# Attention with sinks and a window, then a gated feed-forward: token blocks of the feed-forward re-cut, two groups' attention placed later

## The chip, the cores and the metric

The kernel runs on one core of one Trainium2 chip. The metric is the time of one execution on the device in microseconds (us). Five engines work beside each other, each through its own list of instructions in the order in which it was written: TensorE (PE; its weight loads are shown as PEld), VectorE (DVE), ScalarE (ACT), GpSimd (POOL) and SyncE (SP). Loads that change the type are issued by POOL, transposing transfers and most stores by SP, some stores by ACT.

## The reference

Causal attention over 4 batches, 8 heads, 768 positions, head size 64. A query sees the last 128 positions (its own included) and the first 4, the sinks. The attention's output, 3072 tokens of 512, goes through a gated feed-forward of width 1536.

```python
scores = scale * np.matmul(q, k.transpose(0, 1, 3, 2))
keep = is_sink | in_window            # rel >= 0 and rel < 128, or position < 4
a = np.exp(scores - max); a = a / sum # masked scores are -1e9
x = (a @ v).transpose(0, 2, 1, 3).reshape(B * S, H * D)
g = x @ w_gate
out = (g * sigmoid(g) * (x @ w_val)) @ w_out
```

## The kernel before

**Groups and blocks.** The attention works in 12 *groups* of 256 tokens (three for each batch; group g holds tokens 256 g on). The feed-forward works in 8 *blocks* whose sizes stand in `SIZES` (L42); the first two are gated together. `gate` (L611) is one unit of the first half: a projection `pg` into one PSUM bank (`project`, L564: 4 matmuls of 512 columns, or 8 of 256), its tanh on ACT (L584), a projection `pv` into another bank, then on DVE `u` (L592) and `ht` (L607). A block of 512 has 12 gate units, one of 256 has 6. `down` (L644) is one unit of the second half: 12 matmuls (L657) for 128 tokens, an eviction on ACT (L662) and a store (L665).

**A group's attention.** `load_nat` (L106) brings q and k with four transfers from POOL into a tile of which there is one (`natp`, one buffer); `xbar` (L287) turns them into `kT` and `qT` with four transposing transfers from SP (L293). `step_S1` (L360) writes the scores of all heads into six PSUM banks (L382; 52 matmuls, or 18 for a batch's first group) and, except where it is called "apart", the sinks' scores into a seventh (L432), and has ACT take the exponent of three banks (L395). `step_S2` (L408) takes that of the other three and of the sinks; `step_S1`, `step_S2` and `step_S3` append the four masks, multiplications on DVE (L404), to the list `later`. `step_PV` (L469) multiplies by the values: the first call of a group that has sinks runs `step_sinks` (L447), which opens all four output banks, adds the sinks (L454) and, with L463, the odd parts of the window for all eight heads; every call then adds the main part (L494) and appends a division on DVE (reciprocal L503, product `xn` L511). `step_X` (L523) has SP transpose `xn` into `xT`, the feed-forward's input (L538).

**The order of the work.** The schedule is written by hand: `weave` (L714) runs a list of units and hands each one its attention steps; the numbers in the slots are positions in that list. Within a gate unit, steps marked "ahead" (`step_S1`) come before `pg`, the others between `pg` and `pv`; within a down unit they are spread over its 12 matmuls. `flush` (L241) writes out what `later` holds; in a gate unit `gate_v` (L590) may first put reciprocals, or one mask if it is the first entry, between `u` and `ht`. PSUM has 8 banks, handed out from one pool (L76). POOL's order is kept by `behind` (L701) and `turned` (L705): one-element copies that wait for a transposed tile, so that loads issued behind them start no sooner.

**Around the change.** The first list has 24 units: 12 of gates for blocks 0 and 1, 6 for block 2 (12 to 17), and the downs of blocks 0, 1, 2 (18 to 23). Group 3 is scored at unit 17 and its PVs stand in 19 and 20; group 4 is scored at 19, its PVs stand in 21 and 22. Block 3 (512 tokens) then holds groups 3 and 4; its first two gate units work on 256 tokens each, so that group 4's half may come later. From there on `pair(a, b)` puts two groups into each block's list: a's scores at unit 0, its PVs at 4 and 5, its `step_X` at 7, b's scores at 8, its PVs at 12 and 13, its `step_X` at 13. Block 3 has groups 5 and 6, block 4 has 7 and 8, block 5 has 9 and 10; group 11 is worked while blocks 6 (512) and 7 (256) are gated, and the downs of both follow.

Of the kernel before, what the change touches and what calls it, by code (L numbers as in the profile page):

```python
# [14 lines left out]
def kernel(  # L15
# [12 lines left out]
    nc = tc.nc  # L28
    P = 128
# [9 lines left out]
    NP2 = H // 2  # L39
    GC = S // 256  # L40
    NG = B * GC
    SIZES = [256, 256, 256, 512, 512, 512, 512, 256]  # L42
    assert sum(SIZES) == NTOK and NG == 12
    OFF = [sum(SIZES[:i]) for i in range(len(SIZES))]
    PEX = (0, 1, 2)
# [34 lines left out]
    def bank(shape, dtype, name):  # L80
        return psum.tile(shape, dtype, tag="b", name=name)
# [102 lines left out]
    one = const.tile([P, 1], FP32)  # L184
# [56 lines left out]
    def flush():  # L241
        firsts()
        for f in later:
            f()
        later.clear()
# [274 lines left out]
    def dense(t, c, n):  # L520
        return t[:, 0:c * n].rearrange("p (c n) -> p c n", c=c)

    def step_X(g, j, evict="v"):  # L523
        t0 = g * 256 + j * P
        tb = max(i for i in range(len(SIZES)) if OFF[i] <= t0)
        off = t0 - OFF[tb]
        if tb == 0 and off == 0:
            xTs["01"] = xtp.tile([P, DMC, 512], BF16, tag="xT", name="xT")
            xTs[0], xTs[1] = (xTs["01"][:, :, 256 * i:256 * (i + 1)] for i in range(2))
        elif tb > 1 and off == 0:  # L530
            xTs[tb] = dense(xtp.tile([P, DMC * 512], BF16, tag="xT", name="xT"),
                            DMC, SIZES[tb])
            if tb == 3:
                for i in range(2):
                    xTs[tb, i] = xTs[tb][:, :, 256 * i:256 * (i + 1)]
        if g not in PEX:
            def sp():
                nc.sync.dma_start_transpose(xTs[tb][:, :, off:off + P], xns[g, j])  # L538
            later.append(sp)
            return  # L540
        pt = bank([P, DMC, P], BF16, "px")
        for i in range(DMC):
            nc.tensor.transpose(pt[:, i], xns[g, j][:, i * P:(i + 1) * P], ident)  # L543

        if evict == "a":
            nc.scalar.copy(out=xTs[tb][:, :, off:off + P], in_=pt)
            return

        def dve():
            nc.vector.tensor_copy(out=xTs[tb][:, :, off:off + P], in_=pt)  # L550
        if evict == "now":
            dve()
        else:
            later.append(dve)
# [18 lines left out]
    def new_h(tb):  # L573
        if tb not in hts:
            n = SIZES[tb]
            t = hpool.tile([P, DFC * 512], BF16, tag="ht", name="ht")
# [13 lines left out]
    def gate_v(tb, f, pg, th, pv):  # L590
# [11 lines left out]
        if tb == "01":  # L602
# [4 lines left out]
        nc.vector.tensor_tensor(  # L607
            hts[tb][:, f:f + 512 // SIZES[tb]].rearrange("p a n -> p (a n)"), u, pv,
            op=ALU.mult)
# [23 lines left out]
    def gate_first(tb, f, attn):  # L633

        step_PV(1, 0, 1, "a")
        step_PV(1, 1, 1)
        flush()
        a = gate_a(tb, f)
        step_X(1, 1, "now")
        step_X(1, 0, "a")  # L640
        held.pop()()
        gate_b(tb, f, *a)

    def down(tb, ts, attn, last=False):  # L644
        at = {}
        for i, a in enumerate(attn):
            at.setdefault(DFC * (i + 1) // (len(attn) + 1), []).append(a)
        n = DFC // 4
        r0 = OFF[tb] + ts * P
        parts = [(0, 3 * P), (3 * P, DM)] if last else [(0, DM)]  # L650
        for m, (lo, hi) in enumerate(parts):
            po = bank([P, hi - lo], FP32, "pd")
            for f in range(DFC):
                for a in at.get(f, []) if m == 0 else []:
                    a()
                    flush()
                nc.tensor.matmul(  # L657
                    po, hts[tb][:, f, ts * P:(ts + 1) * P], wos[f // n][:, f % n, lo:hi],
                    start=(f == 0), stop=(f == DFC - 1))
            ot = opool.tile([P, hi - lo], FP32, tag=f"ot{hi - lo}", name="ot")  # L660
            if m == 0:
                nc.scalar.activation(ot, po, AF.Copy, scale=0.5)  # L662
            else:
                nc.vector.tensor_scalar(ot, po, 0.5, None, op0=ALU.mult)  # L664
            (nc.scalar if tb < 3 else nc.sync).dma_start(out[r0:r0 + P, lo:hi], ot)  # L665

    def gates(tb):
        return [(gate, tb, f) for f in range(0, DFC, 512 // SIZES[tb])]

    def downs(tb):  # L670
        return [(down, tb, t) for t in range(SIZES[tb] // P)]

    def A(fn, *a):
        return lambda: fn(*a)

    def TN(g, evict="av"):
        return [A(step_TN, g, i, j, evict) for j in range(2) for i in range(2)]
# [4 lines left out]
    def S1(g, apart=False):  # L682
        f = A(step_S1, g, apart)
        f.ahead = True
        return f

    def one(at, g, apart=False):
        return [(at, [S1(g, apart), A(step_S2, g, apart)]), (at + 1, [A(step_S3, g)])]
# [6 lines left out]
    def PVs(g):  # L695
        return [A(step_PV, g, j, hh) for hh in range(2) for j in range(2)]

    def Xs(g):
        return [A(step_X, g, j) for j in range(2)]
# [14 lines left out]
    def weave(us, slots):  # L714
        assert all(i < len(us) for i in slots)
        for i, (fn, tb, x) in enumerate(us):
            fn(tb, x, slots.get(i, []))

    def slots(*pairs):
        sl = {}  # L720
        for at, steps in pairs:
            for i, step in zip(at if isinstance(at, tuple) else (at,) * len(steps),
                               steps):
                sl.setdefault(i, []).append(step)
        return sl
# [117 lines left out]
    for f in masks1[:3]:  # L843
        f()

    g0, g1, g2 = gates(0), gates(1), gates(2)
    us = [(gate_held, *g0[0][1:]), (gate_first, *g0[1][1:]), g1[0], g1[1],
          *((gate, "01", f) for f in range(4, DFC)),
          *g2, *downs(0), *downs(1), *downs(2)]

    def L(*fs):
        def f():
            for x in fs:
                x()
        return f

    def NV(g):
        return L(A(load_nat, g), A(load_v, g))
# [4 lines left out]
        ((10, 11), [A(step_X, 2, 0, "a"), ahead(A(step_X, 2, 1, "a"))]),  # L863
        (11, [NV(4), lambda: nc.gpsimd.tensor_copy(out=vcl[64:128], in_=vcl[0:64])]),
        ((14, 14, 15, 15), TN(3, "aa")),
        (15, [A(xbar, 4)]), (15, [A(load_nat, 5)]), (19, [A(xbar, 5, (0,))]),
        *one(17, 3), (18, [A(step_ks, 1)]), (18, [A(step_vsb, 1)]),
        ((19, 19, 19, 20), PVs(3)), (19, [S1(4)]), (20, [L(A(step_S2, 4), A(step_S3, 4))]), (20, Xs(3)), (20, [A(xbar, 5, (1,))]),
        ((21, 21, 21, 22), PVs(4)), (21, Xs(4)[:1]),
        (22, [Xs(4)[1], flush, A(behind, 3, 511), A(load_v, 5), A(load_nat, 6)]),  # L870
        (23, [A(xbar, 6), A(turned, 6), A(load_v, 6), NV(7)])))

    def pair(ga, gb, at=0):
        return [*one(at, ga), ((4, 4, 5, 5), PVs(ga)), ((7, 7), Xs(ga)), *one(8, gb, True),
                ((12, 12, 13, 13), PVs(gb)), ((13, 13), Xs(gb))]

    weave([(gate, (3, i), 0) for i in range(2)] + gates(3)[2:] + downs(3), slots(
        (15, [A(step_ks, 2), A(step_vsb, 2)]), *pair(5, 6), (9, [flush, A(xbar, 7)]),
        (13, [flush, A(behind, 4, 511), NV(8)]),
        (15, [A(xbar, 8)]), (15, [NV(9)])))  # L880
    weave(gates(4) + downs(4), slots(
        *pair(7, 8), (3, [A(xbar, 9)]), (15, [A(step_ks, 3), A(step_vsb, 3)]),
        (3, [A(load_nat, 10)]), (13, [flush, A(behind, 5, 511), A(load_v, 10), NV(11)]),
        (15, [A(xbar, 10)])))
    weave(gates(5) + downs(5), slots(*pair(9, 10), (6, [A(xbar, 11)])))
    us = gates(6) + gates(7) + downs(6) + downs(7)
    us[-1] = (lambda tb, t, a: down(tb, t, a, True), *us[-1][1:])
    weave(us, slots(
        *one(0, 11), ((4, 4, 5, 5), PVs(11)), ((8, 9), Xs(11))))


# [33 lines left out]
```

## Time and profile before

| | |
|---|---|
| median of 3 runs | 234.16 us (233.87 to 234.39) |
| profiled execution | 233.82 us |
| its span, first to last instruction | 231.9 us |
| PE / DVE / ACT / POOL busy | 225.6 / 150.9 / 106.4 / 84.3 us |
| gate projections pg and pv, PE (L564) | 74.2 and 74.1 us |
| output projection, PE (L657) | 65.9 us |
| u and ht on DVE (L592, L607) | 49.2 and 42.5 us |
| tanh, and window exponents, on ACT (L584, L395) | 43.7 and 28.5 us |

The span is what lies between the first and the last instruction of the program; the time of an execution has some 2 us more around it. The page gives each engine's busy time, then the span in 40 slices of 5.8 us with a digit for the busy share in tenths, then the chain of work that ended last. The trace behind it answers questions: the timeline of an engine (start, length, what), who waited for whom, and the busy times of a stretch. The busy time of a group of matmuls counts overlapping ends, so the distance from one matmul's start to the next is the better measure.

### The profile page before, as it was taken

How to read it: one execution, taken by the hardware profiler on the slowest of the kernel's cores; microseconds unless marked ns; L12 is line 12 of the kernel's file. 1: busy time of each engine (PE TensorE's matmuls, PEld its weight loads, DVE VectorE, ACT ScalarE, POOL GpSimd, SP SyncE). 2: the span in 40 equal slices, each digit the busy share in tenths (PEclk: the TensorE clock that was granted, in tenths of full speed). 3: DMA queues.
4: the chain of work that ended last, by engine and by line, in shares of the span. 5: the costliest groups of instructions: out<-in, count | busy, mean ns of one | idle time of the engine just before them, and what ended most of it. 6: DMA issues, size and time to landing. Idle time of an engine off the chain costs nothing.

```text
span 231.9 us, 5433 instructions
## 1 busy us (share of the span) xinstructions
PE 225.6 (97%) x2155; PEld 125.4 (54%) x2155; DVE 150.9 (65%) x327; ACT 106.4 (46%) x212; POOL 84.3 (36%) x123
## 2 busy tenths in 40 slices
PE   7699999999999999999999999999999999999994
PEld 3469645796555644455444454454454544487443
DVE  5878888767660797960797970597960599778000
ACT  4784486566543726423635512835612823333221
POOL 8996874960500907806353415135000000000000
PEclk9979999999999999999999999999999999999999
DMA  8999999999998998998989996989915102000132
GB/s 147 150 185 179 179 198 206 164 156 122 123 154 230 103 134 99 151 195 141 146 119 139 128 124 138 105 109 144 117 40 144 45 3 42 3 3 0 64 120 90
DMA packets 112008, 28.04 MB, mean 121 GB/s; under 512 B 99056, under 2 KB 109040, under 8 KB 111984
## 3 DMA queue, kind: packets, MB, share of 16 engines
q0 software_dynamic: 79904, 14.29, 80.7%
q1 hardware_dynamic: 30672, 11.58, 26.7%
q10 hardware_dynamic: 1408, 1.84, 2.5%
q8 instruction: 17, 0.28, 0.5%
q14 instruction: 7, 0.06, 0.1%
HBM read 29.13 MB, written 6.29 MB: 153 GB/s over the span
## 4 chain that ended last, share of the span: by engine, by line
PE 94%; DMA 2%; POOL 2%; DVE 0%; issue 0%; POOLq 0%
PE pg L564 27%; PE pv L564 27%; PE pd L657 27%; PE o L494 4%; PE s L382 3%; DMA rows<-in_q_dram 2%; PE s L326 1%; PE o L463 1%; PE pk L432 1%; PE pn L279 1%; PE o L454 1%; POOL rows L102 1%; POOL x L216 1%; PE px L543 1%; DVE xT L550 0%
## 5 line engine op out<-in xcount | busy, mean ns | idle before, releaser
L592 DVE SCALAR_TENSOR_TENSOR u<-th,pg 128x512 bf16<-128x512 f32 x72 | 49.2, 683 | 45.4 <-ACT th L584 45.1
L564 PE MATMUL pg<-xT,wg 128*128 128x512 bf16 (+1 forms) x360 | 74.2, 337 | 0.3 <-DVE xT L550 0.3
L564 PE MATMUL pv<-xT,wv 128*128 128x512 bf16 (+1 forms) x360 | 74.1, 336 | 0.0
L584 ACT ACTIVATE th<-pg 128x512 f32<-128x512 f32 x72 | 43.7, 608 | 59.6 <-PE pg L564 59.6
L657 PE MATMUL pd<-wo,ht 128*128 128x512 bf16 (+2 forms) x300 | 65.9, 370 | 0.0
L564 PEld LDWEIGHTS <-wg 128*128 128x128 bf16 x360 | 34.4, 98 | 26.7 <-issue 0.7
L564 PEld LDWEIGHTS <-wv 128*128 128x128 bf16 x360 | 33.9, 98 | 23.5 <-issue 0.2
L607 DVE TENSOR_TENSOR ht<-u,pv 128x512 bf16<-128x512 bf16 x62 | 42.5, 686 | 4.7 <-PE pv L564 0.4
L657 PEld LDWEIGHTS <-ht 128*128 128x128 bf16 x300 | 27.5, 98 | 28.4
L662 ACT ACTIVATE ot<-pd 128x512 f32<-128x512 f32 (+1 forms) x24 | 14.3, 595 | 50.2 <-PE pd L657 46.8
L395 ACT ACTIVATE e<-s 128x512 bf16<-128x512 f32 x54 | 28.5, 614 | 5.8 <-PE s L382 4.9
L113 POOL DMA_DIRECT2D nat<-in_k_dram x20 | 17.7, 895 | 29.3 <-DMA qT<-nat 27.8
L511 DVE TENSOR_TENSOR xn<-o,rcp 128x256 bf16<-128x256 f32 x45 | 17.9, 419 | 0.7
L128 POOL DMA_DIRECT2D vm<-in_v_dram x24 | 17.8, 770 | 1.2 <-DMA va<-in_v_dram 0.7
L113 POOL DMA_DIRECT2D nat<-in_q_dram x20 | 17.8, 906 | 1.0 <-DMA wv<-in_moe_w_val_dram 0.5
L494 PEld LDWEIGHTS <-e 128*128 128x128 bf16 x256 | 12.0, 100 | 6.3 <-issue 0.3
L404 DVE TENSOR_TENSOR e<-e,maskq 128x768 bf16<-128x768 bf16 x24 | 13.1, 553 | 1.9 <-ACT e L395 1.9
L151 POOL DMA_DIRECT2D va<-in_v_dram x12 | 10.7, 917 | 4.3 <-DMA wo<-in_moe_w_out_dram 2.4
L703 POOL CAST warmed<-xT 1x1 f32<-1x1 bf16 x3 | 0.5, 175 | 30.2 <-DMA xT<-xn 30.2
L503 DVE RECIPROCAL rcp<-o 128x4 f32<-128x4 f32 x48 | 7.3, 172 | 5.5 <-PE o L494 5.3
L664 DVE TENSOR_SCALAR ot<-pd 128x128 f32<-128x128 f32 x1 | 0.3, 292 | 14.3 <-PE pd L657 14.3
L333 ACT ACTIVATE e<-s 128x512 bf16<-128x512 f32 x16 | 8.3, 607 | 0.6 <-PE s L326 0.5
(86 smaller groups left out, 138.7 us busy)
## 6 DMA issues: line engine op xcount, KB each, us to landing
out_dram<-ot SPq DMA_DIRECT2D x17, 256.0 KB
nat<-in_k_dram POOLq DMA_DIRECT2D x20, 128.0 KB, 4.7
nat<-in_q_dram POOLq DMA_DIRECT2D x20, 128.0 KB, 4.9
va<-in_v_dram POOLq DMA_DIRECT2D x12, 128.0 KB, 5.9
wg<-in_moe_w_gate_dram POOLq DMA_DIRECT2D x6, 256.0 KB, 7.6
wv<-in_moe_w_val_dram POOLq DMA_DIRECT2D x6, 256.0 KB, 8.2
wo<-in_moe_w_out_dram POOLq DMA_DIRECT2D x4, 384.0 KB, 11.1
out_dram<-ot ACTq DMA_DIRECT2D x6, 256.0 KB
```

The costliest lines, as they stand in the source:

```text
L113: nc.gpsimd.dma_start(x[:, i, j].rearrange("p (h d) -> p h d", d=D), src[b, :, t0:t0 + P].rearrange("h p d -> p h d"))
L128: nc.gpsimd.dma_start(vms[b][p0:p1, t - 1, :, 0:D], v[b, :, t0:t0 + p1 - p0].rearrange("h p d -> p h d"))
L395: nc.scalar.activation(e_t[g][:, e0:e0 + 512], pss[g][w, i], AF.Exp, scale=scale)
L404: nc.vector.tensor_tensor(e, e, m.broadcast_to([P, 2, 384]), op=ALU.mult)
L494: nc.tensor.matmul(o, l, r, start=(c == 0 and i == 0), stop=(i == len(mms) - 1), skip_group_check=True)
L511: nc.vector.tensor_tensor(xn, po[:, :, 0:D], rcp.broadcast_to([P, 4, D]), op=ALU.mult)
L564: nc.tensor.matmul(ps[:, i * n:(i + 1) * n], ws[fi][:, c, fo * P:(fo + 1) * P], xTs[tb][:, c], start=(c == 0), stop=(c == DMC - 1))
L584: nc.scalar.activation(th, pg, AF.Tanh, scale=0.5)
L592: nc.vector.scalar_tensor_tensor(u, th, 1.0, pg, op0=ALU.add, op1=ALU.mult)
L607: nc.vector.tensor_tensor(hts[tb][:, f:f + 512 // SIZES[tb]].rearrange("p a n -> p (a n)"), u, pv, op=ALU.mult)
L657: nc.tensor.matmul(po, hts[tb][:, f, ts * P:(ts + 1) * P], wos[f // n][:, f % n, lo:hi], start=(f == 0), stop=(f == DFC - 1))
L662: nc.scalar.activation(ot, po, AF.Copy, scale=0.5)
```

## The change

Block 3 becomes one of 256 tokens with group 3 alone, and the last four blocks have 512 tokens each. The 6 gate units and 2 downs of block 3 join the first list as units 24 to 31. Group 4 is scored at unit 22 (PVs in 25 and 26), group 5 at unit 27 (PVs in 29 and 30). The pairs shift by one group: block 4 has groups 6 and 7, block 5 has 8 and 9, block 6 has 10 and 11, and block 7 has none. Transfers, waits of POOL, and the small steps `step_ks` and `step_vsb` are placed anew; `turned` is no longer called. The split gate units belong to block 4 now. The stores of block 3 are issued by ACT.

```diff
-    SIZES = [256, 256, 256, 512, 512, 512, 512, 256]
+    SIZES = [256, 256, 256, 256, 512, 512, 512, 512]
...
-            if tb == 3:
+            if tb == 4:
...
-            (nc.scalar if tb < 3 else nc.sync).dma_start(out[r0:r0 + P, lo:hi], ot)
+            (nc.scalar if tb < 4 else nc.sync).dma_start(out[r0:r0 + P, lo:hi], ot)
...
-          *g2, *downs(0), *downs(1), *downs(2)]
+          *g2, *downs(0), *downs(1), *downs(2), *gates(3), *downs(3)]
...
-        (15, [A(xbar, 4)]), (15, [A(load_nat, 5)]), (19, [A(xbar, 5, (0,))]),
+        (15, [A(xbar, 4)]), (15, [A(load_nat, 5)]),
         *one(17, 3), (18, [A(step_ks, 1)]), (18, [A(step_vsb, 1)]),
-        ((19, 19, 19, 20), PVs(3)), (19, [S1(4)]), (20, [L(A(step_S2, 4), A(step_S3, 4))]), (20, Xs(3)), (20, [A(xbar, 5, (1,))]),
-        ((21, 21, 21, 22), PVs(4)), (21, Xs(4)[:1]),
-        (22, [Xs(4)[1], flush, A(behind, 3, 511), A(load_v, 5), A(load_nat, 6)]),
-        (23, [A(xbar, 6), A(turned, 6), A(load_v, 6), NV(7)])))
+        ((19, 19, 19, 20), PVs(3)), (20, Xs(3)), (20, [A(xbar, 5)]),
+        (20, [flush, A(behind, 3, 255), A(load_v, 5), A(load_nat, 6)]),
+        *one(22, 4), ((25, 25, 26, 26), PVs(4)), (26, [A(xbar, 6)]), (26, [A(load_v, 6)]),
+        ((27, 28), Xs(4)),
+        *one(27, 5), ((29, 30, 30, 30), PVs(5)), (30, Xs(5)),
+        (30, [flush, A(behind, 4, 511), NV(7)])))
...
-    weave([(gate, (3, i), 0) for i in range(2)] + gates(3)[2:] + downs(3), slots(
-        (15, [A(step_ks, 2), A(step_vsb, 2)]), *pair(5, 6), (9, [flush, A(xbar, 7)]),
-        (13, [flush, A(behind, 4, 511), NV(8)]),
-        (15, [A(xbar, 8)]), (15, [NV(9)])))
-    weave(gates(4) + downs(4), slots(
-        *pair(7, 8), (3, [A(xbar, 9)]), (15, [A(step_ks, 3), A(step_vsb, 3)]),
-        (3, [A(load_nat, 10)]), (13, [flush, A(behind, 5, 511), A(load_v, 10), NV(11)]),
-        (15, [A(xbar, 10)])))
-    weave(gates(5) + downs(5), slots(*pair(9, 10), (6, [A(xbar, 11)])))
-    us = gates(6) + gates(7) + downs(6) + downs(7)
+    weave([(gate, (4, i), 0) for i in range(2)] + gates(4)[2:] + downs(4), slots(
+        (3, [A(step_ks, 2), A(step_vsb, 2)]), *pair(6, 7), (2, [A(xbar, 7)]),
+        (7, [flush, A(behind, 5, 255), NV(8)]), (9, [A(xbar, 8)]),
+        (13, [flush, A(behind, 5, 511), NV(9)]), (15, [A(xbar, 9)])))
+    weave(gates(5) + downs(5), slots(
+        *pair(8, 9), (3, [A(load_nat, 10)]), (6, [A(xbar, 10)]),
+        (13, [flush, A(behind, 6, 511), A(load_v, 10), NV(11)]),
+        (14, [A(step_ks, 3), A(step_vsb, 3)]), (15, [A(xbar, 11)])))
+    weave(gates(6) + downs(6), slots(*pair(10, 11)))
+    us = gates(7) + downs(7)
     us[-1] = (lambda tb, t, a: down(tb, t, a, True), *us[-1][1:])
-    weave(us, slots(
-        *one(0, 11), ((4, 4, 5, 5), PVs(11)), ((8, 9), Xs(11))))
+    weave(us, {})
```

## The prediction

> **What bounds the kernel now.** First the page: busy shares, the slices, the granted clock, then the chain that ended last.
>
> ```profile
> span 231.9 us, 5433 instructions
> ...
> PE 225.6 (97%) x2155; PEld 125.4 (54%) x2155; DVE 150.9 (65%) x327; ACT 106.4 (46%) x212; POOL 84.3 (36%) x123
> ...
> PE   7699999999999999999999999999999999999994
> ...
> PEclk9979999999999999999999999999999999999999
> ...
> PE 94%; DMA 2%; POOL 2%; DVE 0%; issue 0%; POOLq 0%
> ```
>
> TensorE is full in every slice but the first two and the last. A busy PE need not be PE at its peak, so I went on to the timeline of PE and took the time from one matmul's start to the next: 216 ns for 512 columns and 109 ns for 256 (four in 0.86, eight in 0.87). From 17.2 us to the last matmul at 228.75 no start comes more than 0.10 us later than its columns explain, and those 0.10 stand only where the tile of the array changes (into and out of scores, sinks and the odd window parts). The list of waits says the same: after 20 us no PE entry but "issue". So TensorE waits for nothing here, and **a reordering can save nothing after 17 us; it can only open gaps.**
>
> **Matmuls and other work.** Both lists hold four blocks of 256 and four of 512, so the 720 gate and 300 output matmuls keep count and width. Two groups with sinks are scored "apart" before (8, 10) and after (7, 11), so the 0.10 us changes keep their count as well. Nothing before unit 19 changes. The last four output units, the split last tile and its store are the same: the 2.9 us behind the last matmul stay. Sum so far: 0. Everything rests on whether the new order makes PE wait, so I laid the units out with the durations of before, on before's clock.
>
> **Where block 3 starts.** Before, group 5's scores start at 73.68 behind group 4's attention. Take away 0.1 for the tile change and 1.2 for group 4's sinks and PV (65.06 to 65.89, then 3 x 0.13): block 3's gates (unit 24) start at 72.4. A 256-wide gate unit is 1.745; with sinks and two PVs 0.96 more (82.55 to 83.51), with two later PVs 0.25. Unit 25 starts at 74.1, 26 at 76.8, and group 5's step_S1 at 78.8 + 0.1 = **78.9**, right behind the PVs of group 4.
>
> **Gap 1: banks, 78.9.** step_S1 of group 5 and its sink scores take 7 of the 8 PSUM banks, the next pg the eighth. The pool gives the bank free longest (of 90 tiles followed in the program of before, 84 took it and 6 the second). The eight latest tenants are pg and pv of units 25 and 26 and group 4's four PV sums, so the last scores need unit 26's pv and pg27 the last PV sum. DVE frees these in the sequence seen here, in the timeline of DVE where group 5 has its PVs (start, length, engine, line, what):
>
> ```profile
> 84.01 0.68 DVE L592 SCALAR_TENSOR_TENSOR u<-th,pg 128x512 bf16<-128x512 f32 x1
> 84.61 0.24 DVE L503 RECIPROCAL rcp<-o 128x4 f32<-128x4 f32 x2
> 84.79 0.69 DVE L607 TENSOR_TENSOR ht<-u,pv 128x512 bf16<-128x512 bf16 x1
> 85.40 0.75 DVE L511 TENSOR_TENSOR xn<-o,rcp 128x256 bf16<-128x256 f32 x2
> ```
>
> From the start of u the pv is free after 1.47 and the last xn after 2.14. Unit 26's tanh starts 0.2 after its pg ends (77.7) and takes 0.6, so u starts at 78.6, pv is free at 80.07 and the last PV sum at 80.74. The scores need the third pair of banks 0.57 after their start (36 of 52 matmuls, 0.82 us), at 79.5; pg27 would start at 79.95 and starts at 80.8. **Gap 1 is 0.85 us.** Before never had this: pair() leaves two units between PVs and the next scores. Bounds: 0 if the bank order differs kindly, 1.4 if DVE has 0.5 us of backlog.
>
> **Gap 2: masks, 85.7.** Group 5's sinks and PV stand in unit 29, two units behind its scores; pair() leaves four. The loop at L463 reads all eight heads, so it needs the last of the four masks. How long that takes under gates is seen in the timelines of PE, ACT and DVE at group 7's scores:
>
> ```profile
> 108.76 0.89 PE L382 MATMUL s<-qT,kT 64*64 64x192 bf16 x52
> ...
> 109.36 1.57 ACT L395 ACTIVATE e<-s 128x512 bf16<-128x512 f32 x3
> 110.88 0.60 ACT L584 ACTIVATE th<-pg 128x512 f32<-128x512 f32 x1
> ...
> 111.51 0.69 DVE L592 SCALAR_TENSOR_TENSOR u<-th,pg 128x512 bf16<-128x512 f32 x1 [8.34 <-ACT th L584]
> ...
> 115.32 0.55 DVE L404 TENSOR_TENSOR e<-e,maskq 128x768 bf16<-128x768 bf16 x1
> ```
>
> Three exps, tanh, three exps on ACT; then u, mask, ht, mask twice over on DVE. From the end of the tanh (111.48) to the end of the last mask (115.87) it is 4.39; in unit 28 the transpose issue stands ahead of the masks, so u and ht go first, 0.19 more. After the change pg27 ends at 81.67, its tanh at 82.47, the last mask at 87.05. PE gets there at 80.8 + five halves of 0.872 + 0.1 + 0.22 (sinks) + 0.19 (four heads) = 85.67. **Gap 2 is 1.4 us.** It is there without gap 1 as well (84.8 against 86.2). Bounds: 0 if the masks are as quick as group 3's, whose scores start at 52.44 under one last gate unit and whose masks end at 58.13, 5.7 later (PE takes 5.9 without gap 1); 2.1 by the first group 5 (73.68 to 81.31, 7.6, behind a store issue on ACT). I take group 7's row: same engines under gates.
>
> **Transfers.** From the first issue of a nat load to the start of its transposes SP takes 3.8 to 5.5 us (78.05 to 81.85, 90.50 to 95.96), four transposes 5.1, a pair 2.55, landing 1.3 behind the end (74.47, POOL released at 75.79). Laid in the queues' order, on the clock with the gaps: xT of group 3 lands at 64.5, wanted at 72.4; kT and qT of group 5 69.7, wanted 78.9; of group 6 82, wanted 94; xT of group 5 94.6, wanted 96.7; kT and qT of group 7 107, wanted 109.4; v of group 10 170, wanted 173; kT and qT of group 11 177, wanted 180. SP has each next xbar ahead of the X of the group before it, and POOL each next load behind the `behind` wait; dropping `turned` takes a 6.7 us POOL wait that nobody stood behind. All margins are 2 us or more: cost 0, and up to 2 for one load that lands late. step_ks and step_vsb move under gates (0.34 + 0.43 on DVE at block 4's unit 3); DVE had caught up two units later (u at 86.06, straight after its tanh at 86.03), long before group 7's scores: 0, at most 0.8. Two stores move to ACT (0.34 each); the second stands before group 6's first exps, as one did at 74.42 with no gap on PE: 0, at most 0.34.
>
> **Sum.** 0.85 + 1.4 = 2.25, say 2.3. On the profiled execution's own 233.82 (span 231.9 and 1.9 around it) that is 236.1. That execution lies 0.34 under the median of the runs, 234.16, so 236.1 leans low by that much.
>
> **The clock.** Four stretches asked of the trace, two shown: the one half-clock stretch inside the work followed a gappy one.
>
> ```profile
> 8.01:11.42 3.41, 2.26 (x74) 1.71 (x74) 2.55 (x8) 2.57 (x7) 3.28 (x7) 1.00 2.08 164
> 11.42:14.83 3.41, 3.41 (x53) 2.38 (x51) 2.21 (x9) 2.88 (x6) 3.35 (x6) 0.50 1.73 174
> ```
>
> Columns: length, busy time of PE, its loads, DVE, ACT, POOL, then the granted clock. With 2.26 of 3.41 us busy the next 3.41 ran at 0.50, which costs 1.7; with 2.72 busy (4.60 to 8.01) it stayed at 1.00. Gap 2 leaves 2.0 busy if it falls in one such stretch, so the trace allows a halved stretch. The Trainium skill ("TensorE: Matmul & The Clock Gate", "Why this matters for your kernels") warns only of idle gaps over about 3 us; by that the sum stays 2.3, by the row it is 4.0. I keep 2.3 as likeliest: that early stretch also had matmuls of 64 columns on a quarter of the array, unlike the gates around gap 2.
>
> **Rivals.**
> - *The masks and banks come in time* (not slower): DVE and ACT serve group 5 as they served group 3. For it: 5.7 us there. Against: three gate units of DVE work lie around it here, and every masking under gates took 6.9 to 7.6. It decides at 5.9 us from first score to last mask. Price 0 to 0.5: 233.8 to 234.3. Chance 0.13.
> - *Halved clock on top*: 1.7 more, 237.8. Chance 0.15.
> - *A transfer lands late*: POOL's loads for groups 10 and 11 now stand behind `behind` of block 5's second group, and S1 of 11 has 3 us. Beyond that each us late is a us of PE: 238 to 240. Chance 0.08.
> - *Faster*: PE would have to lose 0.5 us of work, which the counts exclude, or the early half-clock stretch would have to fall away, in code that stays: 232.1. Chance 0.06.
>
> The forecast itself has 0.58. That the order is not what the diff says is excluded: the engines keep the written order.
>
> **Range.** The forecast's bounds are 235.0 to 237.3; with the halved clock (238.0) and the upper part of the first rival (from 234.0) about 8 in 10 are held. What a measurement can tell from no change is 0.2%, 0.47 us (233.7 to 234.6): faster 0.06, same 0.13, slower 0.81.
>
> **What will show it.** PE idle before or inside L382 of group 5's scoring (52 matmuls near 79) with DVE as releaser: gap 1. PE idle before L463 some 6 us later, released by DVE e L404: gap 2. If neither shows, the first rival holds. PEclk under 9 in slices 15 to 16: the clock. PE idle at L382 near 109 or 180, released by a DMA: a late transfer. A shorter PE sum of L564, L657 or the attention would make the whole reasoning wrong.

## The result and the profile after

The changed kernel takes 237.31 us (236.58 to 238.26, 6 runs) where the kernel before takes 234.01 (232.92 to 234.55, 6 runs): a ratio of 1.0151, 95% interval 1.0114 to 1.0188. That is 3.3 us slower. The forecast was 236.1, 2.3 above the execution it started from, in a range of 234.0 to 238.0, slower with a chance of 0.81.

The page of the changed kernel, with the same lines as before: span, busy times, PE's slices, granted clock, and the chain by engine.

```profile
span 234.8 us, 5417 instructions
...
PE 225.1 (96%) x2131; PEld 125.4 (53%) x2155; DVE 151.7 (65%) x327; ACT 106.6 (45%) x212; POOL 85.2 (36%) x124
...
PE   7799999999999989998999999999999999999994
...
PEclk9799999999999999999999999999999999999999
...
PE 80%; DMA 8%; POOL 4%; DVE 3%; issue 2%; SPq 2%; ACT 0%; POOLq 0%; DVEq 0%
```

The busy times are those of before (PE 225.1 against 225.6, DVE 151.7 against 150.9), and so are the weight loads (2155, 125.4 us), so no work was added; that PE counts 2131 instead of 2155 is 24 matmuls whose records are missing from this trace. PE's row has an 8 in slices 15 and 19, where before had 9 throughout, and the chain runs through transfers, POOL and DVE for a sixth of the span, where PE had 94% of it. A chain that leaves the engine that was never idle before is the first sign of a new wait. The waits of PE from 20 to 228 us name them (who waited, for whom, us in total, times, longest); the same question to the kernel before gets an empty list.

```profile
PE o L463 <- DVE e L404: 1.1, 2, 0.8
PE s L382 <- DMA qT<-nat: 0.8, 1, 0.8
PE s L382 <- DVE ht L607: 0.5, 1, 0.5
PE pv L564 <- DVE ht L607: 0.3, 1, 0.3
PE pd L657 <- issue: 0.2, 1, 0.2
```

The last line is no wait: of the 20 matmuls of L657 that start near 67.4 the trace has 19, and the gate behind them starts 4.56 us after the sinks' scores ahead of them, as in kernel 5 below, whose trace has all 20. The timeline of PE places the others; the bracket is the idle time before the line and what ended it.

```profile
78.20 0.69 PE L382 MATMUL s<-qT,kT 64*64 64x192 bf16 x35
79.40 0.45 PE L382 MATMUL s<-qT,kT 64*64 64x128 bf16 x17 [0.51 <-DVE ht L607]
79.79 0.30 PE L432 MATMUL pk<-qT,kss 128*32 128x128 bf16 x8
80.02 1.05 PE L564 MATMUL pg<-xT,wg 128*128 128x256 bf16 x8
...
84.71 0.32 PE L463 MATMUL o<-vm,e 64*64 64x65 bf16 x16
85.87 0.22 PE L463 MATMUL o<-vm,e 64*64 64x65 bf16 x4 [0.84 <-DVE e L404]
86.33 0.29 PE L463 MATMUL o<-vm,e 64*64 64x65 bf16 x12 [0.24 <-DVE e L404]
86.56 0.29 PE L494 MATMUL o<-vm,e 128*128 128x65 bf16 x4
...
103.88 0.53 PE L494 MATMUL o<-va,e 128*128 128x65 bf16 x12
104.74 1.02 PE L564 MATMUL pv<-xT,wv 128*128 128x512 bf16 x3 [0.33 <-DVE ht L607]
...
109.97 0.89 PE L382 MATMUL s<-qT,kT 64*64 64x192 bf16 x52 [0.75 <-DMA qT<-nat]
```

The same passages before, at group 5, where PE waits for nothing:

```profile
73.68 0.89 PE L382 MATMUL s<-qT,kT 64*64 64x192 bf16 x52
74.51 0.29 PE L432 MATMUL pk<-qT,kss 128*32 128x128 bf16 x8
74.74 1.05 PE L564 MATMUL pg<-xT,wg 128*128 128x256 bf16 x8
...
82.87 0.45 PE L463 MATMUL o<-vm,e 64*64 64x65 bf16 x32
83.25 0.42 PE L494 MATMUL o<-vm,e 128*128 128x65 bf16 x8
```

The brackets count from the modelled end of the matmul before; from start to start, against the same passage undisturbed, the losses are larger. Group 5's scores stop after 35 matmuls: 1.82 us to the next gate where it was 1.06, 0.76 lost (gap 1). The loop over eight heads stops after four heads, 16 matmuls, and once more after the fifth: 1.85 us where it was 0.38, 1.47 lost (gap 2). The pv in group 6's second PV unit starts 0.86 after the PV matmuls ahead of it, for DVE, where the unit before it needs 0.37: 0.49. Group 7's scores lose 0.85, for a transfer. Together 3.57.

For comparing kernels I use one distance that leaves the start of the program out, because the start alone moved by 0.7 us between the two profiled executions: from the first weight load of group 3's scores to the last matmul. It is 176.31 us before (52.44 to 228.75) and 179.85 after (51.73 to 231.59). The waits above, 3.57, explain all of these 3.54.

### The profile page after: what moved, and what is told of

Its sections match the earlier page's. It is cut to its first block, busy times and chain, and to the rows that moved or that the text cites. A ratio compares the mean times of both kernels' runs of the same rounds, so it can differ in the third digit from the quotient of the medians.

```text
span 234.8 us, 5417 instructions
## 1 busy us (share of the span) xinstructions
PE 225.1 (96%) x2131; PEld 125.4 (53%) x2155; DVE 151.7 (65%) x327; ACT 106.6 (45%) x212; POOL 85.2 (36%) x124
## 4 chain that ended last, share of the span: by engine, by line
PE 80%; DMA 8%; POOL 4%; DVE 3%; issue 2%; SPq 2%; ACT 0%; POOLq 0%; DVEq 0%
PE pd L657 24%; PE pg L564 23%; PE pv L564 23%; PE o L494 3%; PE s L382 3%; DMA qT<-nat 3%; DMA wg<-in_moe_w_gate_dram 2%; DMA nat<-in_k_dram 2%; POOL va L151 1%; DMA xT<-xn 1%; SPq L293 1%; POOL rows L102 1%; PE o L463 1%; DVE ht L607 1%; PE pn L279 1%
## 5 line engine op out<-in xcount | busy, mean ns | idle before, releaser
L657 PE MATMUL pd<-wo,ht 128*128 128x512 bf16 (+2 forms) x290 | 64.5, 370 | 0.6 <-issue 0.2
L657 PEld LDWEIGHTS <-ht 128*128 128x128 bf16 x300 | 27.7, 98 | 28.9
L395 ACT ACTIVATE e<-s 128x512 bf16<-128x512 f32 x54 | 28.5, 612 | 6.5 <-PE s L382 4.6
L404 DVE TENSOR_TENSOR e<-e,maskq 128x768 bf16<-128x768 bf16 x24 | 13.1, 554 | 8.0 <-ACT e L395 8.0
L382 PE MATMUL s<-qT,kT 64*64 64x64 bf16 (+4 forms) x366 | 8.1, 218 | 1.3 <-DMA qT<-nat 0.8
L382 PEld LDWEIGHTS <-kT 64*64 64x64 bf16 (+1 forms) x366 | 6.4, 106 | 4.9 <-issue 4.4
```

Source lines behind the costliest of these rows:

```text
L382: nc.tensor.matmul(pss[g][w, lo // 8][part, 64 * (lo % 8):64 * (lo % 8) + 64 * (hi - lo)], kTs[b][r, p, k0:k0 + kn], qTs[b][r, p, cc:cc + ...
L395: nc.scalar.activation(e_t[g][:, e0:e0 + 512], pss[g][w, i], AF.Exp, scale=scale)
L657: nc.tensor.matmul(po, hts[tb][:, f, ts * P:(ts + 1) * P], wos[f // n][:, f % n, lo:hi], start=(f == 0), stop=(f == DFC - 1))
```

## The experiments

My theory from the prediction: each loss is a wait of TensorE set by how closely steps follow each other (banks for gap 1, masks for gap 2), and the late arrival that the prediction priced at nothing makes the rest. The main rival: the re-cut blocks cost by themselves. All kernels but the tenth start from the changed one; "distance" is the one just defined, from one profiled execution, given as the excess over 176.31. The last column has what PE loses from start to start, each against the same passage undisturbed: gap 1, gap 2, the pv near 104, and group 7's scores with the step to the gate behind them. In every kernel these add up to the distance within 0.03 us. Ratios are to the kernel before, measured on the same chip.

| kernel | ratio (95%) | distance | us lost by PE |
|---|---|---|---|
| changed | 1.0151 (1.0114 to 1.0188) | +3.5 | gap 1 0.76, gap 2 1.47, pv 0.49, scores of 7 0.85 |
| 1 masks of group 5 out | 1.0110 (1.0054 to 1.0166) | +2.1 | gap 1 0.72, pv 0.50, scores of 7 0.86 |
| 2 group 4's PVs sooner | 1.0171 (1.0130 to 1.0212) | +3.6 | gap 1 0.09, gap 2 1.47, pv 0.51, scores of 7 1.58 |
| 3 values of 7 held back | 1.0140 (1.0100 to 1.0180) | +3.4 | gap 1 0.95, gap 2 1.47, pv 0.15, scores of 7 0.85 |
| 4 group 5 scored sooner | 1.0108 (1.0066 to 1.0151) | +1.4 | pv 0.33, scores of 7 0.85, 0.18 at unit 24 |
| 5 = 3 and 8 | 1.0116 (1.0066 to 1.0165) | +2.4 | gap 1 0.71, gap 2 1.47, scores of 7 0.21 |
| 6 = 4 and 8 | 1.0054 (1.0029 to 1.0078) | +0.8 | scores of 7 0.82 |
| 7 = 3, 4 and 8 | 1.0022 (0.9998 to 1.0047) | +1.1 | 0.95 (new place), scores of 7 0.21 |
| 8 step_ks, step_vsb moved | 1.0148 (1.0102 to 1.0193) | +3.4 | gap 1 1.27, gap 2 1.47, scores of 7 0.65 |
| 9 = 7, scored one unit later | 1.0041 (1.0017 to 1.0066) | +1.5 | 0.41 and 0.93 (new), scores of 7 0.21 |
| 10 old kernel, PVs sooner | 1.0086 (1.0056 to 1.0116) | +1.8 | 1.79 in L463 |
| 11 = 9, its two waits out | 1.0014 (0.9984 to 1.0045) | +0.3 | scores of 7 0.21, and 0.1 for one more change of the array's tile |

The changed kernel and kernels 1, 3, 5 and 8 have the same code up to gap 1, and gap 1 is 0.71 to 1.27 in them. So one execution of the same code differs from the next by up to 0.6 us there, and a difference of a few tenths between two distances says nothing by itself.

**1. Group 5's masks left out.**

```diff
 def masks(g, w, x):
...
+        if g == 5:
+            return
```

> Leaves out the four masks of group 5 (DVE), nothing else: the window of that group is not cut, so its output is not the reference's. My theory: TensorE's wait inside L463 near 85 (1.00 + 0.43 us in the changed kernel's trace) is for the last masks, so it goes; 237.3 falls by 1.2 to 1.5, to 235.8 to 236.1, and the wait inside L382 near 78.7 (0.67) stays. Rival: the sinks' exponents or the values, not the masks, set that wait, or another wait takes its place at the next half-block gate: 237.0 to 237.3.

The wait in L463 is gone and the one in L382 stays; the distance falls by 1.5. The time against before falls by 0.4% (1.0110), some 1.0 us, with wide intervals. So the masks set gap 2, as the row of group 7 had said.

**2. Group 4's PVs a unit sooner.**

```diff
-        *one(22, 4), ((25, 25, 26, 26), PVs(4)),
+        *one(22, 4), ((24, 24, 25, 25), PVs(4)),
```

> PVs of group 4 one unit sooner (24, 24, 25, 25), so that unit 26 lies between them and group 5's scores. My theory: the wait inside L382 near 78.7 (0.67 us) is for banks that the unit just before still holds (its pv and the last PV sums); with a unit between, the eight latest tenants are older and the wait goes: 236.5 to 236.8, with the wait in L463 still there at 1.3 to 1.5. Rival: DVE is simply behind at that point, whichever tile holds the banks: the wait stays above 0.4 and the time within 0.2 of 237.3.

Half right. Gap 1 is gone: group 5's scores run through, 0.09 is left. But the time did not fall, and the timeline of PE shows where it went:

```profile
78.26 0.89 PE L382 MATMUL s<-qT,kT 64*64 64x192 bf16 x52
...
85.23 0.22 PE L463 MATMUL o<-vm,e 64*64 64x65 bf16 x4 [0.84 <-DVE e L404]
...
110.10 0.89 PE L382 MATMUL s<-qT,kT 64*64 64x192 bf16 x52 [1.51 <-DMA qT<-nat]
```

TensorE came to group 7's scores 0.7 sooner and waited there that much longer; they start at 110.10, as in the changed kernel (109.97). The chain into that transfer goes back through POOL to xT of group 5, and POOL's copy that waits for it did come 0.63 sooner (93.86 against 94.49). From there to the landing of group 7's last q transpose, by the last update of its semaphore, it was 16.1 us in this execution and 14.7 to 15.4 in the others that have the value loads there (changed, 1, 4, 6, 8). So the size and the cause of gap 1 are shown. That removing it alone gains nothing is what this execution and the ratio of four runs say; a transfer that landed late took the gain back here, and that it always does is not shown.

**3. The values of group 7 held back.** POOL's five value loads wait, by a one-element copy, for the q transposes; the copy also tells when these land.

```diff
-        (30, [flush, A(behind, 4, 511), NV(7)])))
+        (30, [flush, A(behind, 4, 511), A(load_nat, 7)])))
...
-        *pair(6, 7), (2, [A(xbar, 7)]),
+        *pair(6, 7), (2, [A(xbar, 7), A(turned, 7), A(load_v, 7)]),
```

> Group 7's value loads (five, 98.8 to 102.7 in the changed kernel) held back behind a one-element copy that waits for group 7's q transposes. Theory A, crowding: those transposes were issued by 104.8 and landed only at 110.0 because the value loads lay beside them; held back, they land 1.5 to 3 us after their issue, and the wait before group 7's scores (0.8 us near 109) goes: 236.4 to 236.7. Theory B, lateness: the nat loads themselves start too late (95.3, behind the wait for group 5's xT): the wait stays within 0.3 of 0.8 and the time within 0.3 of 237.3.

SP's transposes in the changed kernel, then POOL's copy in this one (start, length, idle before and what ended it):

```profile
101.75 3.07 SPq L293 DMA_TRANSPOSE qT<-nat  x2
```

```profile
106.66 0.17 POOL L709 CAST warmed<-qT 1x1 f32<-1x1 bf16 x1 [7.97 <-DMA qT<-nat]
```

Issued by 104.82, the q transposes let the scores go at 109.97 in the changed kernel, 5.1 later. Here they were issued by 105.07 and had landed at 106.66, 1.6 later. So crowding it was, for the landing, and the other kernels say the same: by the last update of its semaphore the last q transpose landed 3.0 to 5.0 us after its issue in the six with the loads there (changed, 1, 2, 4, 6, 8), and 1.2 to 1.5 in the five without (3, 5, 7, 9, 11). The Trainium skill ("Trainium Kernel Development and Optimization", "Key Constraints") says that transfers of SP's, ACT's and POOL's queues run on the same 16 engines and interleave; these landings agree. But the loss at the scores stayed at 0.85: in place of the transfer they now waited for DVE.

```profile
109.75 0.45 PE L382 MATMUL s<-qT,kT 64*64 64x128 bf16 x17 [0.40 <-DVE ht L607]
```

That is gap 1's pattern, banks held by the units just before. Neither of my two theories had it.

**4. Group 5 scored sooner.**

```diff
-        *one(22, 4), ((25, 25, 26, 26), PVs(4)),
+        *one(22, 4), ((26, 26, 27, 27), PVs(4)),
...
-        ((27, 28), Xs(4)),
-        *one(27, 5), ...
+        ((28, 28), Xs(4)),
+        *one(24, 5), ...
```

> Group 5's scores at unit 24 in place of 27 and group 4's PVs at 26 and 27 in place of 25 and 26; everything else as changed. My theory, that both waits come from how closely group 5's steps follow each other and group 4's: five units lie between its scores and its PV, and its scores find banks that the downs gave back long ago, so both waits go (0.67 + 1.43): 235.0 to 235.4, with the wait before group 7's scores still there. Rival, that the cost is in the blocks' re-cut and not in the places: 236.8 to 237.3.

Gaps 1 and 2 are gone and the distance falls by 2.2, the sum of both (0.76 + 1.47). The time, 1.0108, is 1.0 us less than the changed kernel's by ratio, not 2.1; its runs spread from 234.89 to 237.44. What is left stands at group 7's scores, and DVE ends it. The timeline of DVE in this kernel shows why it is behind there:

```profile
100.04 0.69 DVE L607 TENSOR_TENSOR ht<-u,pv 128x512 bf16<-128x512 bf16 x1
100.65 0.52 DVE L299 COPY kss<-kT 64x16 bf16<-64x16 bf16 x2
101.18 0.43 DVE L304 TENSOR_TENSOR vsb<-vcl,diag_h 128x260 bf16<-128x260 f32 x1
101.52 0.68 DVE L592 SCALAR_TENSOR_TENSOR u<-th,pg 128x512 bf16<-128x512 f32 x1
...
107.80 0.69 DVE L607 TENSOR_TENSOR ht<-u,pv 128x512 bf16<-128x512 bf16 x1
108.41 0.68 DVE L592 SCALAR_TENSOR_TENSOR u<-th,pg 128x512 bf16<-128x512 f32 x1
```

No line has an idle time in brackets: DVE works without a pause from 94.9 to 109.9, and step_ks and step_vsb put 0.87 into it.

**8 and 5. step_ks and step_vsb moved, alone and with the values held back.**

```diff
-        (30, [flush, A(behind, 4, 511), NV(7)])))
+        (30, [flush, A(behind, 4, 511), NV(7)]), (31, [A(step_ks, 2), A(step_vsb, 2)])))
...
-        (3, [A(step_ks, 2), A(step_vsb, 2)]), *pair(6, 7), (2, [A(xbar, 7)]),
+        *pair(6, 7), (2, [A(xbar, 7)]),
```

Kernel 5 has this and the diff of kernel 3.

> step_ks and step_vsb of batch 2 (0.34 to 0.69 and 0.43 us on DVE) moved from block 4's gate unit 3 to the last down of block 3, where DVE is idle; nothing else. Theory, two waits stacked before group 7's scores: DVE is behind there by what these steps take, but the transfer lands later still. The 0.3 us wait near 104 (pv for ht) goes, TensorE comes to group 7's scores sooner and waits there for the q transposes as much longer: time within 0.3 of 237.3, a ratio to before of 1.013 to 1.016. Rival, DVE alone: 0.6 to 1.1 less, a ratio near 1.011.

> The value loads of group 7 held back as in the run before, and step_ks and step_vsb moved as in the other run of this set. Theory, two waits stacked: both are gone together, so group 7's scores start straight behind the gates and nothing waits between 88 and 112; 0.8 + 0.3 us less than the changed kernel, and the two waits of group 5 stay: a ratio to before of 1.009 to 1.011. Rival, a third wait takes their place (the banks, or the held back values at group 7's PVs): a ratio of 1.013 or more, and TensorE waits near 109 or 118.

Two waits stood on one spot. At group 7's scores PE loses 0.85 in the changed kernel, 0.85 with the values held back, 0.65 with the small steps moved, and 0.21 with both. Whole distances hide this: they fall by 0.14, 0.16 and 1.17, but gap 1, ahead of both edits, happened to be larger in kernels 3 and 8 (0.95 and 1.27 against 0.76). From the start of group 6's scores to the gate behind group 7's it is 17.63 us in the changed kernel, 17.28 in kernel 3, 16.94 in kernel 8 and 16.50 in kernel 5, so each edit does gain alone, 0.35 and 0.69, and most of that at the pv near 104. In kernel 8 the loss there is gone and the scores wait 0.6 for the transposes; I had expected that wait to grow to about 1.1, but the transposes landed 0.6 sooner in this execution. The ratio of kernel 5 (1.0116) lies above the 1.009 to 1.011 that I gave, its interval holds both; no wait but group 5's two and 0.2 at the pg behind group 7's scores is left in its trace.

**6 and 7. All repairs with the new blocks**, without and with the values held back (the diffs of 4 and 8, and in 7 that of 3 too).

> Group 5's scores at unit 24, group 4's PVs at 26 and 27, and step_ks and step_vsb in the last down of block 3; group 7's value loads where the change has them. Theory: waits of group 5 gone, DVE's backlog before group 7 gone, and what is left is the crowded landing of group 7's q transposes, 0 to 0.9 us near 107: a ratio to before of 1.000 to 1.005. Rival, that the re-cut itself costs: 1.008 or more.

> All three repairs with the new blocks: group 5's scores at unit 24 and group 4's PVs at 26 and 27, step_ks and step_vsb in the last down of block 3, group 7's value loads held back. Theory, that the change cost only through these waits and that TensorE's work is a floor: no wait of 0.2 us or more after 20 us, ratio to before 0.998 to 1.003. Rival, that four blocks of 512 at the end or the re-cut cost by themselves: 1.006 or more. A ratio under 0.997 would say that the new order saves work, which the counts exclude.

Kernel 6 has one wait of 0.75 left, for group 7's transposes; its ratio of 1.0054 lies just outside the 1.000 to 1.005 of my theory and below its rival's. Kernel 7 is at 1.0022, inside; but one wait was new, where I had expected none:

```profile
72.90 0.89 PE L382 MATMUL s<-qT,kT 64*64 64x192 bf16 x52 [0.88 <-DMA qT<-nat]
```

Scored at unit 24, group 5 finds its q transposes not yet landed, issued by 69.14 beside its own three value loads; they landed at 72.77. Kernels 4 and 6 have the same code up to there, and theirs landed at 72.16 and 71.87, just in time for scores at 72.29 and 72.46. So this wait comes in some executions and not in others: at unit 24 there is no time to spare.

**9. Group 5 scored at unit 25** (`one(25, 5)` in kernel 7).

> The repaired order with the new blocks once more, with group 5's scores at unit 25 in place of 24 (in the run before, TensorE waited 0.9 us at unit 24 for group 5's q transposes in the profiled execution). Theory, the re-cut is free and every loss was a wait: no wait of 0.3 us or more after 20 us, ratio to before 0.998 to 1.002. Rival: a cost of the blocks themselves stays, 1.003 or more with no wait to show for it.

A miss. The ratio is 1.0041, and there were waits to show for it:

```profile
73.84 0.89 PE L382 MATMUL s<-qT,kT 64*64 64x192 bf16 x52 [0.34 <-DMA qT<-nat]
75.59 0.30 PE L432 MATMUL pk<-qT,kss 128*32 128x128 bf16 x8 [0.86 <-DVE u L592]
```

The transposes are still late (landed at 73.70), and the sinks' scores, which need a seventh bank in the middle of gates, wait for the pg of the unit before.

**11. Both of these taken away.**

```diff
-        (20, [flush, A(behind, 3, 255), A(load_v, 5), A(load_nat, 6)]),
+        (20, [flush, A(behind, 3, 255), A(load_nat, 6), A(load_v, 5)]),
...
-        *one(25, 5), ...
+        *one(25, 5, True), ...
```

> The run before (group 5's scores at unit 25) with its two remaining waits taken away: group 5's sink scores behind pg (apart), so that they need no seventh bank at once, and group 5's value loads issued behind group 6's nat loads, which themselves wait for group 5's transposes. Theory, the re-cut costs nothing and every loss was a wait: the waits near 73.5 (0.34, for q transposes) and 74.5 (0.86, for a bank) go, no wait of 0.3 us or more from 20 us on, ratio to before 0.999 to 1.002. Rival: the blocks themselves cost, 1.003 or more with no wait to show. A ratio under 0.998 would mean the floor that I read from the matmul spacing is none.

The ratio is 1.0014 (0.9984 to 1.0045). From 20 to 228 us the list of PE's waits has one line, the missing record near 67 once more, and the span is that of before (231.9):

```profile
PE pd L657 <- issue: 0.2, 1, 0.2
```

```profile
span 231.7 us, 5415 instructions
```

The distance exceeds that of before by 0.3: 0.2 at the pg behind group 7's scores and 0.1 for one more change of the array's tile. With the new blocks kept and the waits gone, nothing measurable is left: the re-cut itself costs nothing that these runs can see (the interval ends at 0.45%). Nor is it a gain: no kernel here was faster than the one before. That the transposes came in time is not shown to be the work of the moved loads: with no load from POOL beside it the last q transpose landed at 72.22, 3.3 us after its issue, and with the three value loads beside it the other ten took 2.1 to 4.2. So the crowding shown for group 7 is not shown for group 5, and what sets these landings stays open.

**10. The old kernel with one distance shortened.**

```diff
-        ... *pair(5, 6), (9, [flush, A(xbar, 7)]),
+        ... *one(0, 5), ((2, 2, 3, 3), PVs(5)), ((7, 7), Xs(5)), *one(8, 6, True),
+        ((12, 12, 13, 13), PVs(6)), ((13, 13), Xs(6)), (9, [flush, A(xbar, 7)]),
```

> The kernel before, old blocks, with one thing moved: the first PVs of group 5 two units behind its scores (units 2 and 3 of block 3 in place of 4 and 5). Theory, the distance from scores to PV sets the wait, whatever the blocks: TensorE reaches the fourth pair of heads in L463 5.9 us after the first score, the last mask ends 7.1 to 7.6 after it, so a wait of 1.2 to 1.7 us inside L463 near 80 and a ratio of 1.005 to 1.0075. Rival, that the wait belongs to the new blocks (256-wide gates, DVE backlog from group 4): no wait over 0.3 us there, 0.998 to 1.002.

```profile
78.99 0.51 PE L463 MATMUL o<-vm,e 64*64 64x65 bf16 x17 [0.19 <-DMA vm<-in_v_dram]
80.34 0.29 PE L463 MATMUL o<-vm,e 64*64 64x65 bf16 x12 [0.84 <-DVE e L404]
```

Gap 2 appears in the old blocks: the loop at L463 takes 2.17 us there instead of 0.38. The longest stop is for the masks, with some in front of it for group 5's values, which had always had time. The ratio is 1.0086 (1.0056 to 1.0116), above the 1.005 to 1.0075 that I gave, its interval overlapping. The distance from scores to PV sets the wait, whatever the blocks.

## Why the prediction was right, and where it was not

- **TensorE is the bound and can only be made to wait**: right. PE's work did not change (2155 weight loads, 125.4 us, before and after), every kernel's excess is the sum of its waits, and of eleven variants none came out below the kernel before.
- **Block 3's start**: I had 72.4, it came at 71.7 in an execution whose start ran 0.7 sooner.
- **Gap 1, 0.85**: 0.76, and 0.71 to 1.27 over the five kernels that have it, by the releaser named (ht of the unit before). Kernel 2 removes it by one more unit between, as pair() has it. What I missed is that a wait taken away need not be a gain: in kernel 2 a later transfer took it back.
- **Gap 2, 1.4**: 1.47, released by DVE e L404 as said; kernel 10 makes it in the old blocks, kernel 1 unmakes it. Of the rows offered, group 7's was the one to take.
- **Transfers, priced at 0**: this step failed. I took 1.3 us from the end of the transposes' issue to their landing from a place with no loads beside them (74.47 to 75.79, and that was xT), and so had group 7's landing at 107 with 2.4 to spare; with its value loads beside them they took 5.0 and came 0.8 late. The trace of before could have warned me: the last q transposes in it landed 1.2 to 3.9 us after their issue. I had priced each us of lateness at a us of PE and named PE idle at L382 near 109 as its sign, but gave it a chance of 0.08 and reasoned about groups 10 and 11, where it did not come.
- **step_ks and step_vsb, priced at 0 with 0.8 as the bound**: this failed too. It was 0.49 near 104, and another 0.6 hidden behind the transfer (0.85 at the scores in kernel 3, 0.21 in kernel 5). The step said that DVE catches up two units later. That was read at group 5, whose sinks and PVs hold PE for 0.96 us in which DVE can catch up; group 6 has no sinks, its first PVs hold PE for 0.37, and DVE had not caught up. That this difference is the reason is my reading, not tried.
- **The sum**: 2.3 by the prediction. Gaps 1 and 2 came to 2.2, the two terms priced at 0 to 1.3. That the time lies inside the range is in part luck: the range reached to 238.0 for a halved clock that did not come, and waits that the sum had at 0 filled that room.
- **The clock**: the halved stretch did not follow gap 2. The stretches of the changed kernel, then two of kernel 2 around its wait of 1.5 us (columns as in the prediction):

```profile
4.57:7.98 3.41, 2.31 (x41) 1.28 (x35) 2.81 (x9) 2.48 (x7) 3.41 (x5) 1.00 1.32 147
7.98:11.39 3.41, 3.25 (x73) 2.20 (x73) 3.00 (x10) 2.62 (x6) 3.33 (x6) 0.50 2.07 158
83.07:86.48 3.41, 2.33 (x50) 1.65 (x48) 3.31 (x7) 1.35 (x4) 0.00 (x0) 1.00 0.80 133
86.48:89.89 3.41, 3.36 (x45) 2.22 (x39) 2.64 (x9) 0.00 (x0) 0.00 (x0) 1.00 0.15 30
```

```profile
106.62:110.03 3.41, 1.97 (x10) 0.69 (x7) 3.31 (x9) 0.61 (x2) 0.00 (x0) 1.00 1.24 123
110.03:113.44 3.41, 3.34 (x71) 1.83 (x72) 1.57 (x4) 2.85 (x6) 1.06 (x3) 1.00 0.20 38
```

With 2.31 of 3.41 us busy at the start the next stretch went to 0.50; with 2.33 around gap 2, and with 1.97 in kernel 2, it stayed at 1.00. So PE's busy time in the trace does not decide it alone; what does, these runs leave open. Nor do the runs bear out the 1.7 us that I had given a halved stretch: of the executions of the kernel before that ran beside these experiments, the 45 with a mean granted clock of 0.998 or more have a median of 233.2 us, the 25 with 0.993 or less one of 233.9. One halved stretch of 3.41 us leaves 0.993, so it goes with some 0.7 us.

## What to carry to other kernels

Where one engine is full, read a reordering by distances: for each step that moves, the time from its first input to its last reader's need, taken from a place under the same load, against the time at which the full engine gets there. Price a transfer's landing with what will lie beside it in the queues, not from a quiet place. Expect waits to stand on one spot: taking one away can show nothing there until the other is gone too, so remove them together once before calling any of them cheap. And compare the stretch that an edit can reach, from start to start: a whole distance also holds what an earlier wait happened to do in that execution.

## What the runs showed of the hardware that was not expected

The last of group 7's four transposing transfers landed 1.2 to 1.5 us after the end of its issue in the five kernels where no value load from POOL lay beside it, and 3.0 to 5.0 in the six with five such loads. Two copies of 64 x 16 on DVE (kss) in front of group 7's scores took 0.34 together in the seven kernels where POOL issued no load beside them (3, 5 to 9, 11), and 0.69, 0.42, 0.69 and 0.52 in the changed kernel and kernels 1, 2 and 4, where it did; in these four the first copy ended within 0.01 us of the end of POOL's last load (102.67, 101.13, 102.05, 100.99). Kernel 3, which only moves these loads away, has 0.34 in the same place, so the loads made the copies longer. And the half-clock stretch at the start came at 11.42 in the profiled execution before, at 7.98 in the changed one, at 8.23 in kernel 4, and not at all in several others (kernel 7's trace has none before the last matmul), with PE gaps of under 1 us in the stretch ahead of it. The Trainium skill ("TensorE: Matmul & The Clock Gate", "Why this matters for your kernels") ties it to idle gaps of over about 3 us; these rows do not agree, and the measurement decides.
